# Retention with low-rank expert outputs: one load on another queue, the output weights behind other GpSimd work, and the order of the last unit

## The chip, the cores and the metric

The kernel runs on one core of a Trainium2 chip. Its engines are TensorE (PE in the profile; PEld is its weight loading), VectorE (DVE), ScalarE (ACT), GpSimd (POOL) and SyncE (SP). SP, ScalarE and GpSimd can each issue DMA transfers from their own queue. The metric is the device time of one execution, in microseconds, as the median of several runs; lower is better.

## The reference

There are eight batches (B), eight heads (H), 576 positions (S), head width 64. The first half is attention with a fixed decay instead of a softmax:

```python
scores = scale * np.matmul(q, k.transpose(0, 1, 3, 2))
Dmat = np.where(rel >= 0, gamma[:, None, None] ** rel[None, :, :], 0.0)
ret = scores * Dmat[None, :, :, :]
return np.matmul(ret, v).astype(np.float32)
```

The heads of a position are put side by side into rows x of 512. The second half routes each of the 4608 rows to its two best of eight experts, by `x @ w_gate`, weighs the two by a softmax over their two logits, and adds `weight * (x @ A[e]) @ B[e]` to x. A[e] is 512 x 16 and B[e] is 16 x 512.

## The kernel before

**Tiling.** The sequence is cut into four chunks of 128 positions (NFULL = 4) and one of 64. Since the decay is a power of gamma, the work inside a chunk is a masked product, and what came from earlier chunks is a state P (64 x 64 for each head), which is multiplied by a constant gdec from chunk to chunk. A *unit* is one chunk of two batches with all heads; a *quad* is two units (four batches), and q, k and v of a quad are loaded together by `issue`. There are 18 units, 16 full ones and two of the short chunk. h and n are the last two.

**Stages.** Each unit goes through stages with one-letter names. T transposes q and k on TensorE (result pqT and pkT in PSUM, copied to qT and kT). S multiplies k and q (ps) and applies the mask (rt). Q adds what the state gives, R the product with v (px), and scales it with asc to xT, the attention output, transposed. U forms the new state from scaled k and v (pu, P). Z multiplies xT with AW, which holds the 128 columns of all A[e] and the 8 gate columns (pz), and finds the largest logits on DVE (m, ns). V is a sigmoid on ScalarE (sg). W picks and weighs the two experts (cm, then zc). X transposes zc (pzt, zT). B transposes xT back into the output bank (po). Y adds zT times Bcat, the output weights, to po, copies po to osb and issues the output DMAs.

**What sets the order.** `mm`, `vec` and `act` pass each instruction to `chain` (L73), which writes a fixed program order for PE, DVE and ACT. GpSimd's instructions and the DMAs of SP are not chained: a planner orders them by when they are ready in its own model, with the program's order as priority. PSUM has eight banks, which the kernel hands out itself from a list, oldest first (`bank`, `done`).

**The opening (L227 to L241, L650 to L674).** For the first quad, unit 0's q comes from SP's queue and its k from ScalarE's, one batch each; then v and A (Arow), then unit 1's q, k and v, all from SP (L233). `first_T` transposes unit 0. GpSimd scales k (`scale_k`, L259), builds a selection matrix pick in four dependent steps (`fill_pick`, L622), builds asc[0] and issues two loads: the gate columns of AW[0] (L655) and Bcat (L671). Bcat is converted from fp32 to fp16 by the DMA. ScalarE copies asc[0] into asc[1] with the halves swapped, and expands gdec from its packed form. `place_A` brings A into the layout of AW[0] by matmuls with pick, and GpSimd copies AW[0] into AW[1] with the row halves swapped (L670), once A and the gate columns are both in AW[0]. Stage Z uses AW[0] for its first half and AW[1] for its second. TensorE's order behind `place_A` is: T of unit 1 (q, then k), Z of unit 0, S of unit 1, then U, Q and R of unit 1.

**The end (L764 to L777).** The last two units are short. For n, stage Z is run in two halves, (0,) and (1,), and between them stands Y of h, with its four matmuls, its four copies (two on ScalarE, two on DVE) and its four output DMAs of 128 KB from SP. W of n calls V for a half that has none yet. Y of n, also in halves, issues two of its output DMAs from SP and two from ScalarE.

Of the kernel before, what the change touches and what calls it, by code (L numbers as in the profile page):

```python
# [18 lines left out]
def kernel(  # L19
# [10 lines left out]
    nc = tc.nc  # L30
    B, H, S, Dh = q.shape
# [54 lines left out]
    def act(fn, **kw):  # L86
        chain("act", getattr(nc.scalar, fn)(**kw))  # L87
# [107 lines left out]
    def issue(n):  # L195
        if n >= len(quads):
            return
        c, qd = quads[n]
        first = n == 0
        tl = [  # L200
            iop.tile([128, QUAD, H, Dh], FP32, tag=tag, name=tag, bufs=n)
            for tag, n in (("q32", 2), ("k32", 3), ("v32", 3))
        ]
        if c == NFULL:
            if qd > 0:
                return
            for src, dst in zip((q, k, v), tl):
                for g in range(2):
                    nc.sync.dma_start(
                        out=dst[64 * g : 64 * g + 64].rearrange("p s h d -> p (s h) d"),  # L210
                        in_=src[HALF * g : HALF * g + HALF, :, C * c : C * c + L, :].rearrange(
                            "s h j d -> j (s h) d"
                        ),
                    )
            for u in range(2):
                nat[(c, u, 0)] = [x[:, 2 * u : 2 * u + 2] for x in tl]
            return

        def load(n, lo, hi, eng=nc.sync):
            eng.dma_start(  # L220
                out=tl[n][:, lo:hi].rearrange("p b h d -> p (b h) d"),
                in_=(q, k, v)[n][
                    QUAD * qd + lo : QUAD * qd + hi, :, C * c : C * c + C, :
                ].rearrange("b h j d -> j (b h) d"),
            )

        if first:  # L227
            for b in range(2):
                load(0, b, b + 1)
                load(1, b, b + 1, nc.scalar)  # L230
            load(2, 0, 2)
            load_A()
            for n in range(3):  # L233
                load(n, 2, 4)
        else:
            for n in range(3):
                load(n, 0, 4)
        for sl in range(2):
            nat[(c, qd, sl)] = [x[:, 2 * sl : 2 * sl + 2] for x in tl]
# [7 lines left out]
    def rows(g):  # L247
        return slice(64 * g, 64 * g + 64)
# [4 lines left out]
    def scale_k(t):  # L253

        if not is_full(t):
            return
        kk = nat[units[t]][1]
        for b in range(2):
            gp.tensor_tensor(  # L259
                out=kk[:, b],  # L260
                in0=kk[:, b],
                in1=gv[:, 0].unsqueeze(2).broadcast_to((128, H, Dh)),
                op=ALU.mult,
            )
# [30 lines left out]
    def first_T():  # L295

        s = st.setdefault(0, {})
        for nm in ("qT", "kT"):
            s[nm] = wk.tile([128, 2, HP, C], FP32, tag=nm, name=nm, bufs=4 if nm == "qT" else 2)
        for b in range(2):  # L300
            for n, nm in enumerate(("qT", "kT")):
                src = nat[units[0]][n]
                ps = [bank([128, HP, L], f"p{nm}") for _ in range(2)]
                for hp in range(HP):
                    for g in range(2):
                        mm(
                            ps[g][:, hp, :],
                            lhsT=src[rows(g), b, 2 * hp : 2 * hp + 2, :],
                            rhs=id64[rows(g), :],
                            is_transpose=True,  # L310
                            start=True,
                            stop=True,
                        )
                for g in range(2):
                    o = s[nm][:, b, :, rows(g)]
                    if n == 0:
                        act("copy", out=o, in_=ps[g])
                    else:
                        vec("tensor_copy", out=o, in_=ps[g])
                done(*ps)  # L320
# [146 lines left out]
    def stage_B(t):  # L467

        s = st[t]
        po = [bank([128, 2, HP, Dh], f"po{cc}") for cc in range(2)]  # L470
        for g in range(2):
            for dt in range(HP):
                for cc in range(2):
                    mm(
                        po[cc][:, g, dt, :],
                        lhsT=s["xT"][g][rows(cc), dt, :],
                        rhs=id64[rows(cc), :],
                        is_transpose=True,
                        start=(g == 0 and dt == 0),
                        stop=False,  # L480
                        skip_group_check=True,
                    )
        s["po"] = po
# [136 lines left out]
    def fill_pick(*dts):  # L620
        for dt in dts:
            gp.affine_select(  # L622
                out=pick, in_=pick, compare_op=ALU.not_equal, fill=1.0, base=128 * dt,
                pattern=[[-1, 4], [1, 128]], channel_multiplier=-4,
            )
# [21 lines left out]
    for t in range(NU):  # L647
        if units[t][2] == 0:
            issue(quads.index(units[t][:2]) + 2)
        if t == 0:  # L650
            spin(10)
            first_T()
            scale_k(0)
            fill_pick(3)
            gp.dma_start(  # L655
                out=AW[0][:, :, ER : ER + E], in_=moe_w_gate.rearrange("(t p) e -> p t e", p=128)
            )
            for ho in range(2):
                act("copy", out=asc[1][rows(ho)], in_=asc[0][rows(1 - ho)])
            act(  # L660
                "copy", out=gdec.rearrange("p a b d -> p a (b d)"),
                in_=gde.unsqueeze(2).broadcast_to((128, HP, 2 * Dh)),
            )
            stage_S(0)
            stage_U(0)
            stage_Q(0)
            stage_R(0)
            place_A()
            for ho in range(2):
                gp.tensor_copy(out=AW[1][rows(ho)], in_=AW[0][rows(1 - ho)])  # L670
            gp.dma_start(out=Bcat, in_=moe_B.rearrange("e r d -> (e r) d"))  # L671
            stage_T(1, ("qT",))
            stage_T(1, ("kT",), shared=True)
            scale_k(1)  # L674
            stage_Z(0)
            stage_S(1)
            stage_W(0)
            stage_U(1)
            stage_Q(1)
            stage_R(1)  # L680
            stage_T(2, ("qT",))
            stage_B(0)
            stage_X([0])
            stage_Z(1)
            stage_V(1)
            stage_Y(0, spread=True)
            stage_T(2, ("kT",), shared=True)
            stage_T(3)
            scale_k(2)
            scale_k(3)  # L690
            stage_S(2)
            stage_W(1)
            stage_S(3)
            for u in (2, 3):
                stage_U(u)
                stage_Q(u)
                stage_R(u)
            late_T(4)
            for ho in range(2):
                gp.tensor_tensor(  # L700
                    out=maskh[ho], in0=trih.unsqueeze(1).broadcast_to((128, HP, L)),
                    in1=heads(1, ho, L), op=ALU.mult,
                )
            continue
        if t < 4 or units[t][2] or not is_full(t):
            continue

        before, near = [u for u in (t - 4, t - 3) if u > 0], (t - 2, t - 1)
        here = (t, t + 1)
        for u in here:  # L710
            for b, nm in enumerate(("qT", "kT")):
                stage_S(u, (b,))
                if t > LATE:
                    stage_T(u + 2, (nm,))
            if t > LATE:
                scale_k(u + 2)
        for u in before:
            stage_B(u)
        stage_X(before)
        stage_Z(near[0])  # L720
        stage_V(near[0])
        for u in before:
            stage_Y(u)
        stage_Z(near[1])
        stage_V(near[1])
        if units[t][0] > 0:
            for u in here:
                stage_Q(u)
        for u in near:
            stage_W(u)  # L730
        for u in here:
            stage_U(u)
            if units[t][0] == 0:
                stage_Q(u)
            stage_R(u)
        if t <= LATE:
            late_T(t + 2)
# [28 lines left out]
    stage_X([h])  # L766
    stage_Z(n, (0,))
    stage_V(n, (0,))
    stage_Y(h, spread=True)
    stage_Z(n, (1,))  # L770
    for g in range(2):
        stage_W(n, (g,))
    stage_B(n)
    for g in range(2):
        stage_X([n], (g,))
# [30 lines left out]
```

## Time and profile before

| | |
|---|---|
| median of 8 runs | 185.66 us (184.83 to 187.32) |
| the profiled execution | 187.32 us, span 185.6 us |
| granted TensorE clock, mean over the span | 0.987 |
| busy: PE, PEld, DVE, ACT, POOL | 176.5, 164.9, 115.3, 66.8, 58.2 us |
| DMA | 38.74 MB, mean 209 GB/s |

The span runs from the first to the last instruction; what the execution takes besides (1.7 us here) lies around it. The busy time of an engine counts its instructions, not its waits. In a row of the timeline the columns are start, length, engine, source line, operation, output from inputs, number of instructions; a bracket at its end gives the idle time of the engine before it and what is taken to have ended that. Matmuls, vector and scalar instructions have one line each (L81, L84, L87), since three helpers issue them; they are told apart by their tiles. A row with q behind the engine's name (SPq, ACTq) is the issuing of a DMA from that queue. The rows of DMA issues give the size and the median time from issue to landing.

### The profile page before, as it was taken

To read this page: it belongs to the slowest core of one execution; us is meant where nothing else is said; L and a number is where in the kernel's file an instruction comes from. 1 tells how busy PE (TensorE), PEld (TensorE's weight loads), DVE (VectorE), ACT (ScalarE), POOL (GpSimd) and SP (SyncE) were. 2 spreads that over 40 slices of the span, in tenths; PEclk is the share of its full clock that TensorE was granted. 3 is DMA by queue.
4 is the path that set the end of the run, shared out by engine and by line. 5 is a ranking of instruction groups with operands and counts; after the bars stand their busy time and mean duration, and the time that the engine had idled before them with its cause. 6 is when DMAs were issued, how large, how long until landed. Compare 5 with 4: busy or idle time off the path is not lost. (4 is left out here: it accounts for less than half of the span.)

```text
span 185.6 us, 8103 instructions
## 1 busy us (share of the span) xinstructions
PE 176.5 (95%) x3606; PEld 164.9 (89%) x3606; DVE 115.3 (62%) x294; ACT 66.8 (36%) x179; POOL 58.2 (31%) x69
## 2 busy tenths in 40 slices
PE   7996999999999999999999999999999999999970
PEld 2796998999999999999999999999999999999850
DVE  3784565997578745866267716792578447475660
ACT  3512127024412434097602643075406460132440
POOL 8785106226016600688022710443050004000000
PEclk9998799999999999999999999999999999999998
DMA  6999999997998897899897699999800050033175
GB/s 138 278 255 216 274 271 265 262 309 224 250 280 248 228 295 213 232 350 287 237 316 246 188 296 336 229 215 194 280 4 0 4 222 11 4 112 123 66 247 144
DMA packets 53283, 38.74 MB, mean 209 GB/s; under 512 B 26992, under 2 KB 48640, under 8 KB 53248
## 3 DMA queue, kind: packets, MB, share of 16 engines
q1 hardware_dynamic: 50688, 37.23, 70.7%
q10 hardware_dynamic: 2384, 0.85, 1.9%
q8 instruction: 28, 0.46, 1.0%
q0 software_dynamic: 176, 0.15, 0.5%
q14 instruction: 7, 0.06, 0.1%
HBM read 28.91 MB, written 9.44 MB: 207 GB/s over the span
## 5 line engine op out<-in xcount | busy, mean ns | idle before, releaser
L84 DVE TENSOR_TENSOR rt<-ps,mask 128x512 f32<-128x512 f32 x64 | 40.3, 683 | 9.5 <-PE ps L81 9.2
L259 POOL TENSOR_TENSOR k<-k,pack 128x512 f32<-128x512 f32 x32 | 32.6, 1045 | 27.6 <-PE pkT L81 21.0
L81 PE MATMUL pz<-AW,xT 128*128 128x136 f32 x288 | 38.6, 288 | 0.0
L418 POOL TENSOR_TENSOR P<-pn,gdec 128x512 f32<-128x512 f32 x12 | 15.3, 1279 | 68.7 <-DVE pn L84 64.5
L81 PEld LDWEIGHTS pz<-AW,xT 128*128 128x128 f32 x288 | 35.9, 196 | 0.2
L81 PE MATMUL ps<-qT,kT 64*128 64x128 f32 x512 | 34.2, 280 | 0.1
L81 PEld LDWEIGHTS ps<-qT,kT 64*128 64x128 f32 x512 | 31.0, 189 | 1.3 <-issue 0.9
L81 PE MATMUL px<-rt,v 128*64 128x128 f32 x512 | 30.7, 273 | 0.0
L87 ACT COPY qT<-pqT 128x512 f32<-128x512 f32 (+1 forms) x33 | 16.8, 568 | 31.8 <-PE pqT L81 31.6
L81 PEld LDWEIGHTS px<-rt,v 128*64 128x64 f32 x512 | 27.7, 137 | 0.0
L84 DVE TENSOR_TENSOR xT<-px,asc 128x512 f32<-128x512 f32 x36 | 24.4, 688 | 3.9 <-PE px L81 2.6
L87 ACT COPY kT<-pkT 128x512 f32<-128x512 f32 x29 | 16.0, 600 | 27.5 <-PE pkT L81 18.8
L84 DVE COPY lg<-pz 128x16 f32<-128x16 f32 x17 | 2.9, 173 | 34.3 <-PE pz L81 34.3
L81 PE MATMUL pu<-v,k 128*64 128x64 f32 x512 | 18.1, 224 | 0.0
L87 ACT COPY osb<-po 128x256 f32<-128x256 f32 x60 | 17.5, 386 | 1.4 <-PE po L81 0.8
L87 ACT ACTIVATE sg<-lg,ns 128x8 f32<-128x8 f32 x34 | 8.4, 293 | 26.4 <-DVE ns L84 26.1
L81 PEld LDWEIGHTS pu<-v,k 128*64 128x64 f32 x512 | 16.6, 138 | 1.4 <-issue 1.0
L81 PE MATMUL pkT<-id,k 64*128 64x64 f32 x288 | 12.9, 227 | 1.8 <-DVE qT L84 1.4
L81 PE MATMUL px<-qT,P 64*64 64x128 f32 (+1 forms) x512 | 14.1, 259 | 0.0
L81 PEld LDWEIGHTS pkT<-id,k 64*128 64x128 f32 x288 | 11.4, 141 | 2.9 <-DVE qT L84 1.5
L84 DVE TENSOR_TENSOR pn<-pu,P 128x512 f32<-128x512 f32 x12 | 8.3, 692 | 8.3 <-PE pu L81 8.3
L81 PEld LDWEIGHTS px<-qT,P 64*64 64x64 f32 x512 | 12.5, 133 | 0.9
(54 smaller groups left out, 150.5 us busy)
## 6 DMA issues: line engine op xcount, KB each, us to landing
out_dram<-osb SPq DMA_DIRECT2D x32, 256.0 KB, 3.8
v<-in_v_dram SPq DMA_DIRECT2D x4, 512.0 KB, 7.7
q<-in_q_dram SPq DMA_DIRECT2D x3, 512.0 KB, 5.8
k<-in_k_dram SPq DMA_DIRECT2D x3, 512.0 KB, 7.9
out_dram<-osb SPq DMA_DIRECT2D x6, 128.0 KB, 2.3
q<-in_q_dram SPq DMA_DIRECT2D x2, 256.0 KB, 4.2
k<-in_k_dram ACTq DMA_DIRECT2D x2, 256.0 KB, 4.8
Arow<-in_moe_A_dram SPq DMA_DIRECT2D x1, 256.0 KB, 6.5
```

What stands on the lines that cost most here:

```text
L81: chain("pe", nc.tensor.matmul(*args, **kw))
L84: chain("dve", getattr(nc.vector, fn)(**kw))
L87: chain("act", getattr(nc.scalar, fn)(**kw))
L259: gp.tensor_tensor(out=kk[:, b], in0=kk[:, b], in1=gv[:, 0].unsqueeze(2).broadcast_to((128, H, Dh)), op=ALU.mult,)
L418: nc.gpsimd.tensor_tensor(out=Pt, in0=pn, in1=gdec, op=ALU.mult)
```

## The change

Three things are changed.

1. Unit 1's k is loaded from ScalarE's queue, chained behind ScalarE's copies of `first_T`, instead of from SP between q and v. The expansion of gdec goes from ScalarE to GpSimd, in the program ahead of the last step of pick.
2. The two AW[1] copies and the load of Bcat are chained on GpSimd in this order.
3. In the last unit, the second half of Z and its V come directly behind the first; W of both halves follows, and Y of h comes behind these, ahead of B of n.

```diff
         def load(n, lo, hi, eng=nc.sync):
-            eng.dma_start(
+            return eng.dma_start(
...
             load(2, 0, 2)
             load_A()
-            for n in range(3):
-                load(n, 2, 4)
+            load(0, 2, 4)
+            load(2, 2, 4)
+            nat["k of unit 1"] = lambda: chain("act", load(1, 2, 4, nc.scalar))
...
             spin(10)
             first_T()
+            nat["k of unit 1"]()
             scale_k(0)
+            gp.tensor_copy(
+                out=gdec.rearrange("p a b d -> p a (b d)"),
+                in_=gde.unsqueeze(2).broadcast_to((128, HP, 2 * Dh)),
+            )
             fill_pick(3)
...
                 act("copy", out=asc[1][rows(ho)], in_=asc[0][rows(1 - ho)])
-            act(
-                "copy", out=gdec.rearrange("p a b d -> p a (b d)"),
-                in_=gde.unsqueeze(2).broadcast_to((128, HP, 2 * Dh)),
-            )
...
             for ho in range(2):
-                gp.tensor_copy(out=AW[1][rows(ho)], in_=AW[0][rows(1 - ho)])
-            gp.dma_start(out=Bcat, in_=moe_B.rearrange("e r d -> (e r) d"))
+                chain("pool", gp.tensor_copy(out=AW[1][rows(ho)], in_=AW[0][rows(1 - ho)]))
+            chain("pool", gp.dma_start(out=Bcat, in_=moe_B.rearrange("e r d -> (e r) d")))
...
     stage_Z(n, (0,))
     stage_V(n, (0,))
-    stage_Y(h, spread=True)
     stage_Z(n, (1,))
+    stage_V(n, (1,))
     for g in range(2):
         stage_W(n, (g,))
+    stage_Y(h, spread=True)
     stage_B(n)
```

## The prediction

> **What bounds the kernel now.** I read the engine totals first, then the opening by order of time, the granted clock by window, the transfers' landing times, and the tail by order of time. The totals:
>
> ```profile
> PE 176.5 (95%) x3606; PEld 164.9 (89%) x3606; DVE 115.3 (62%) x294; ACT 66.8 (36%) x179; POOL 58.2 (31%) x69
> PEclk9998799999999999999999999999999999999998
> ```
>
> TensorE is busy for 176.5 of 185.6 us, and the list of its waits leaves little to win outside both ends: between 15.84 and 178.9 us its only idle entry is one of 0.28. The clock row dips once, in the fourth and fifth slices (13.9 to 23.2 us). So a change pays by what it does to the first 21 us, or after 177 us. The opening:
>
> ```profile
> 7.84 2.01 SPq L220 DMA_DIRECT2D k<-in_k_dram  x1
> ...
> 9.47 0.64 POOL L622 TENSOR_SCALAR_AFFINE_SELECT pick<-pick 128x512 f32<-128x512 f32 x1
> ...
> 10.06 0.94 POOL L655 DMA_DIRECT2D AW<-in_moe_w_gate_dram  x1
> ...
> 11.01 0.65 POOL L622 TENSOR_SCALAR_AFFINE_SELECT pick<-pick 128x512 f32<-128x512 f32 x1
> 11.59 0.57 POOL L671 DMA_DIRECT2D Bcat<-in_moe_B_dram  x1
> ...
> 13.69 0.71 PE L81 MATMUL pqT<-id,q 64*128 64x64 f32 x16
> ...
> 15.84 0.71 PE L81 MATMUL pkT<-id,k 64*128 64x64 f32 x16 [1.44 <-DVE qT L84]
> 16.03 1.31 POOL L670 COPY AW<-AW 64x544 f32<-64x544 f32 x2 [2.65 <-DMA AW<-in_moe_w_gate_dram]
> ...
> 16.48 3.17 PEld L81 LDWEIGHTS pz<-AW,xT 128*128 128x128 f32 x16
> ```
>
> TensorE stands still from 14.40 to 15.84 before unit 1's k transposes. The row names DVE's qT copies, but by the code's bank list pkT takes the two banks that unit 0's px gave back at 13.40 us (end of the xT copies). What lands then is k itself:
>
> ```profile
> k<-in_k_dram SPq DMA_DIRECT2D x1, 512.0 KB, 7.9
> ```
>
> Issued at 7.84, landed at 7.84 + 7.9 = 15.74. Its q lands at 6.94 + 4.9 = 11.84. After the gap the clock falls:
>
> ```profile
> 16.50:17.00 0.50, 0.50 (x6) 0.50 (x5) 0.41 (x1) 0.44 (x1) 0.46 (x2) 1.00 1.04 156
> ...
> 18.00:18.50 0.50, 0.50 (x4) 0.50 (x4) 0.00 (x0) 0.00 (x0) 0.50 (x2) 0.50 1.06 352
> ```
>
> (Window and its length; us of PE, PEld, DVE, ACT, POOL; clock; DMA share; GB/s.) It is 0.50 from about 17.0 to 20.4. Unit 0's sixteen pz matmuls take 3.49 us there and 2.07 at full clock for unit 1: 1.42 lost, some 1.5 with the first ps.
>
> **Start, k on ScalarE's queue.** The issue comes behind the qT copies, which end at 7.75: not earlier than the 7.84 of before. What changes is the ring. The nearest row is unit 0's second k, also from ScalarE's queue beside a backlog on SP: issued 1.85, landed after 5.4. That gives 13.2 for k. The Trainium skill speaks against this edit ("DMA: Bandwidth & Descriptors", Issuing engines are not separate DMA queues): all queues share the same DMA engines and interleave. The DMA share is 1.0 to 1.3 here, so the trace agrees that k's bytes come out of q's share: q, 2.0 us of transfer behind k at worst, lands at up to 13.9 instead of 11.84, against a first use at 13.69. By the row both transposes are done at 13.9 + 2 x 0.71 = 15.3, often a little sooner; if the rule meant no gain at all, k would land at 15.7 as before. The sum below hardly depends on which, because of the next edit. ScalarE pays an issue of 0.9 (the same size on SP) to 2.0 us; the asc copies (1.25) end by 11.1 against a use near 12.6. If that cover failed, unit 0's second xT would be late. SP issues v about 2 us sooner, behind the same bytes: nothing.
>
> **Start, gdec on GpSimd.** ScalarE loses 0.62; it was idle until 13.77, so nothing is gained. GpSimd's copy takes about 0.63 (64x544 took 0.636). Its place matters. GpSimd has no written order, and its rows show what the planner does: pick steps, which depend on each other, alternate with something ready (asc, k, k, then the gate weights' load between the last two picks). gdec, always ready and in front of that load in the program, takes that slot; then the last pick is ready and also in front. So I expect pick 9.47, gdec 10.1, pick 10.7, gate load at 10.06 + 0.63 + 0.64 = 11.3. gdec is there for unit 0's P at 11.26, with 0.5 to spare. The load:
>
> ```profile
> AW<-in_moe_w_gate_dram POOLq DMA_DIRECT2D x1, 16.0 KB, 5.8
> ```
>
> It lands at 11.3 + 5.8 = 17.1. All of pz(0) waits for it, and its second half for the two AW copies behind it (1.31), at 18.5. Before, it landed at 15.86 and had 0.6 us of cover under the k transposes; that cover is gone. So the wait for k turns into a wait for the gate weights, from 15.3 to 17.2, and pz starts 0.7 later than 16.48. The bounds: if the planner puts the load where it was, pz can start at 16.0 (0.5 gained); with one more ring to share, 6.5 instead of 5.8 makes it 1.4 lost. I take 0.7.
>
> **The clock.** The Trainium skill ("TensorE: Matmul & The Clock Gate", Part 1) wants an idle window of about 3.4 us for the drop, so by it neither 1.44 nor 2 us of standing would cost anything, and the new start would run at full clock: 1.5 less, partly eaten by the AW copies (first half 17.2 to 18.2, second 18.5 to 19.6). The row has the drop after 1.44 us; with the transposes on both sides it is 13.69 to 16.48, 2.8 us without an ordinary matmul (2.2 us of bare transposes at 40.03 cost no clock). After the change the stretch is 13.7 to 17.2, 3.5 us, so I keep the drop. Then pz takes 3.5 again, ending at 20.7 against 19.97, and the AW copies hide under its slow first half. Start: +0.7.
>
> **Bcat later.** It frees 128 KB of transfers before 18 us and asks for them later. Issued behind the AW copies at 18.5, it lands at 19.1 + 6.3 = 25.4; first use was 28.14. It holds GpSimd for 0.57, so unit 1's k scaling ends at 18.5 + 0.57 + 2.04 = 21.1, needed by pu at 22.14 + 0.7. Zero; if both covers failed, under 1 us.
>
> **Tail.** Before:
>
> ```profile
> 177.35 0.76 DVE L84 COPY osb<-po 128x256 f32<-128x256 f32 x2
> 177.37 0.27 ACT L87 ACTIVATE sg<-pz,ns 128x8 f32<-128x8 f32 x1 [0.81 <-PE po L81]
> 177.54 0.64 ACT L87 COPY osb<-po 128x256 f32<-128x256 f32 x2
> 177.93 4.21 SPq L606 DMA_DIRECT2D out_dram<-osb  x6
> ...
> 178.28 0.17 DVE L84 MAX8 m<-pz 128x8 f32<-128x8 f32 x1 [0.17 <-PE pz L81]
> ...
> 179.30 0.29 DVE L84 TENSOR_TENSOR zc<-pz,cm 128x128 f16<-128x128 f32 x1
> ...
> 181.67 0.50 ACTq L606 DMA_DIRECT2D out_dram<-osb  x1
> ```
>
> Four po matmuls (0.44 of PE) leave the front of the last pz, which then ends at 177.80, not 178.24. DVE, in its written order: m at 177.83, ns, two pairs of cm and zc at 0.25 a step: last zc ends at 179.1, not 179.59. The compute chain gains some 0.3 us behind ScalarE's two copies. But Y(h) carries four output DMAs, and they move with it: DVE's two osb copies now stand behind zc, and the first ends at 179.5, not 177.77. SP issued its six at 177.93, 178.53, 179.27, 179.86, 180.66 and 181.67: about 0.63 apart when nothing holds it. From 179.55 the sixth starts at 179.55 + 5 x 0.63 = 182.7 and lands 2.5 later (its landing before), 185.2. The last landing before is ScalarE's, 181.67 + 2.8 = 184.47. So +0.7. Below: if SP issues at its fastest row (0.35, the pair at 176.31) the end is the compute chain, -0.3. Above: these eight transfers of 128 KB ran at some 210 GB/s; all queued from 179.55, 5 us of transfer after 1.1 of start-up ends near 185.7, +1.2. I take +0.7, the row of the same transfers.
>
> **Sum.** The profiled execution took 187.32 (span 185.6, 1.7 around it): 187.32 + 0.7 + 0.7 = 188.7. It lies 1.66 above the median of 185.66, and the eight runs reach from 184.83 to 187.32. My reading is that the clock loss of 1.5 is not in every run of before; with the longer gap it will be in most runs of after. So I take off 1.0, not 1.66: **187.7 us**.
>
> **Rivals and chances.** One run to the next a kernel like this moves by about 1%, and less than that can't be told from no change.
> - Forecast, 0.58: 187.7, own range 186.6 to 189.0.
> - The gate load keeps its place, 0.25. For: gdec might fill GpSimd's idle 5.5 to 6.9. Against: the planner took k there. pz starts 0.5 sooner, the clock loss comes half the time (-0.7), tail +0.7: 186.8 on the profile's scale, 185.6 on the median's with 1.2 off.
> - k does what is meant and nothing follows, 0.09, the faster side. The one mechanism is unbroken TensorE work from q's transposes into pz: 1.44 + 1.5 gone, and the tail's 0.3: 187.32 - 3.2 = 184.1, which has no clock loss left to take off. It decides from a gate landing at 15.1 or sooner; no row shows one under 5.8 us.
> - Two windows of lost clock and SP at the upper bound, 0.08: 187.7 + 1.5 = 189.2.
> - The change does not bring k sooner: possible by the skill's rule, same time as the forecast.
>
> Slower than 187.52 are about two thirds of the forecast and the fourth case, 0.48; faster than 183.8 half of the third at best, 0.05. The range leaves out a tenth on each side: 184.8 to 189.2.
>
> **What would show it.** Right: the gate load issued after gdec and the last pick, near 11.3; an idle entry of TensorE at pz(0), 1.5 to 2.2 us, with DMA AW named; clock 0.50 behind it; SP's first output of Y(h) near 179.5 plus the shift of the start, and SP's last landing as the end. Wrong: a gate load before 10.5, a full clock through 21 us, or SP's last issue within 0.3 of ScalarE's.

## The result

The changed kernel takes 186.73 us (median of 11 runs, 185.89 to 190.93); the kernel before, run beside it and with the earlier runs 32 times in all, 184.89 us (183.92 to 187.32). The ratio is 1.0097, with a 95% interval of 1.0064 to 1.0130: slower by 1%, some 1.8 us. The profiled execution of the changed kernel took 186.92 us with a span of 185.2. That its span is 0.4 shorter than the 185.6 of before says little: the profiled execution of before was, at 187.32, the slowest of its 32 runs. It had the clock loss behind the opening, and this one has not. So the two traces are compared stretch by stretch here.

The totals and the clock row of the changed kernel's page:

```profile
PE 175.0 (94%) x3606; PEld 163.1 (88%) x3606; DVE 115.8 (63%) x294; ACT 66.2 (36%) x178; POOL 58.8 (32%) x70
...
PEclk9999999999999999999999999999999999999995
```

The same matmuls; TensorE's busy time is 1.5 less, since the clock stayed up behind the opening (unit 0's pz and unit 1's ps are busy for 2.35 and 2.06 us here, 3.49 and 2.31 before). The opening by order of time:

```profile
7.00 0.37 ACTq L220 DMA_DIRECT2D k<-in_k_dram  x1
...
9.39 0.64 POOL L623 TENSOR_SCALAR_AFFINE_SELECT pick<-pick 128x512 f32<-128x512 f32 x1
...
9.97 0.61 POOL L656 COPY gdec<-pack 128x512 f32<-128x512 f32 x1
10.53 0.64 POOL L623 TENSOR_SCALAR_AFFINE_SELECT pick<-pick 128x512 f32<-128x512 f32 x1
...
11.11 0.94 POOL L661 DMA_DIRECT2D AW<-in_moe_w_gate_dram  x1
...
14.43 0.67 PE L81 MATMUL pkT<-id,k 64*128 64x64 f32 x16
...
16.56 1.16 PE L81 MATMUL pz<-AW,xT 128*128 128x136 f32 x8 [1.46 <-DMA AW<-in_moe_w_gate_dram]
...
17.83 0.59 POOL L673 DMA_DIRECT2D Bcat<-in_moe_B_dram  x1
17.94 0.99 PEld L81 LDWEIGHTS pz<-AW,xT 128*128 128x128 f32 x8 [0.41 <-POOL AW L672]
...
19.06 2.06 PE L81 MATMUL ps<-qT,kT 64*128 64x128 f32 x32
```

The wait before the k transposes is gone: k was there, 5.3 us after its issue at 7.00, and pkT follows pqT at 14.43. In its place stands a wait of 1.46 before pz(0), for the gate columns. GpSimd does gdec and the last pick step ahead of their load, which is issued at 11.11 instead of 10.06. pz(0) starts at 16.56; before, it was 16.48. The second half of pz waits once more, for the copies into AW[1]: from the first pz to unit 1's ps it is 2.50 us (16.56 to 19.06), against 2.05 (16.34 to 18.39) in the run with Bcat alone below, which has neither this wait nor the clock loss.

The tail by order of time:

```profile
174.29 2.07 PE L81 MATMUL pz<-AW,xT 128*128 128x136 f32 x16
...
177.43 0.29 DVE L84 TENSOR_TENSOR zc<-pz,cm 128x128 f16<-128x128 f32 x1
...
177.90 1.09 DVE L84 COPY osb<-po 128x256 f32<-128x256 f32 x3 [0.17 <-issue]
...
178.38 3.79 SPq L607 DMA_DIRECT2D out_dram<-osb  x6
...
179.12 1.36 ACTq L607 DMA_DIRECT2D out_dram<-osb  x2
179.34 0.42 DVE L84 COPY osb<-po 128x256 f32<-128x256 f32 x1 [0.36 <-PE po L81]
```

And of before, the two rows that the comparison needs besides those shown ahead:

```profile
175.73 1.15 PE L81 MATMUL pz<-AW,xT 128*128 128x136 f32 x8
...
181.27 0.37 ACT L87 COPY osb<-po 128x256 f32<-128x256 f32 x1 [0.79 <-PE po L81]
```

Both halves of n's Z are now one row of sixteen. Counted from the first pz of n, the last osb copy ends after 5.47 us (179.76 - 174.29), where it was 5.91 (181.64 - 175.73): the computing is 0.44 faster. But the first output of h is issued 4.09 after that point (178.38) instead of 2.20 (177.93), and the span ends after 10.91 us instead of 9.87: the tail is 1.04 longer.

### The profile page after: what moved, and what is told of

It reads as the page before. It is cut to its first block, busy times and chain, and to the rows that moved or that the text cites. A ratio compares the mean times of both kernels' runs of the same rounds, so it can differ in the third digit from the quotient of the medians.

```text
span 185.2 us, 8103 instructions
## 1 busy us (share of the span) xinstructions
PE 175.0 (94%) x3606; PEld 163.1 (88%) x3606; DVE 115.8 (63%) x294; ACT 66.2 (36%) x178; POOL 58.8 (32%) x70
## 5 line engine op out<-in xcount | busy, mean ns | idle before, releaser
L81 PE MATMUL pz<-AW,xT 128*128 128x136 f32 x288 | 37.3, 282 | 1.7 <-DMA AW<-in_moe_w_gate_dram 1.5
L81 PEld LDWEIGHTS pz<-AW,xT 128*128 128x128 f32 x288 | 34.7, 190 | 2.1 <-ACT kT L87 1.6
L81 PEld LDWEIGHTS pkT<-id,k 64*128 64x128 f32 x288 | 11.3, 141 | 1.7 <-DMA k<-in_k_dram 0.7
```

The lines of the kernel that those rows point to most:

```text
L81: chain("pe", nc.tensor.matmul(*args, **kw))
```

## The experiments

"Before" in the ratios is the kernel before, run on the same chip beside each. Ratios with their intervals are compared, not medians, since the chips differ by some tenths of a microsecond.

**The tail alone.** The kernel before with

```diff
-    stage_Y(h, spread=True)
     stage_Z(n, (1,))
+    stage_V(n, (1,))
     for g in range(2):
         stage_W(n, (g,))
+    stage_Y(h, spread=True)
```

> The kernel before with the change's tail alone (opening as before). Theory of the output queue: the four output DMAs of Y(h) start some 1.7 us later against the start of the last Z, SP issues six at 0.6 to 0.65 us apart, and the last landing moves out by about 1.1 us although the last osb copy is some 0.4 us sooner: 1.1 us over the kernel before. Rival, that the whole loss sits in the opening: 0.3 to 0.4 us under the kernel before, with the last landing from ScalarE's queue.

Measured: 1.0053 (1.0015 to 1.0090), 1.0 us. In its trace the span ends 10.92 us after the first pz of n, as in the change. So the tail carries about half of the loss.

**The opening alone.** The change with the tail of before:

> The change with the tail of before put back (opening as changed). Theory of the gate weights: TensorE has no wait before unit 1's k transposes any more but one of about 1.5 us before pz(0), named after the load of AW; against the kernel before 0.4 to 0.8 us slower, 1.1 us faster than the change. Rival, that k on ScalarE's queue brings its gain and the tail alone costs: 1 us or more faster than before.

Measured: 1.0039 (1.0011 to 1.0068), 0.7 us. Together the two halves give 0.92%, the change 0.97%. The wait for the gate columns was there, but only 0.30 in this trace, not 1.5: the load was issued at 10.96 and landed after 4.5 us. The landing differs from execution to execution (below).

**Is it who issues the outputs?** The change with two of h's four outputs issued by GpSimd instead of SP:

```diff
-                q_ = nc.scalar if last and x == 1 else nc.sync
+                q_ = (nc.scalar if last else gp if t == NU - 2 else nc.sync) if x == 1 else nc.sync
```

> The change with h's two output DMAs of the second batch issued by GpSimd instead of SP, so that SP issues four at the end and not six. Theory of the output queue: SP's last issue starts near 180 us of a span like the change's and not 181.6, the end follows the last osb copy, and 1.0 to 1.4 us come back. Rival, that the transfers and not the issues are the limit (about 1 MB at some 210 GB/s from the first start): within 0.4 us of the change.

Measured: 1.0117 (1.0060 to 1.0175, from six runs), no faster than the change. The tail by order of time, then by windows (window and its length; us of PE, PEld, DVE, ACT, POOL; clock; DMA share; GB/s):

```profile
180.01 3.20 SPq L607 DMA_DIRECT2D out_dram<-osb  x4
...
180.54 1.12 POOL L607 DMA_DIRECT2D out_dram<-osb  x2 [22.19 <-ACT osb L87]
...
180.75 1.37 ACTq L607 DMA_DIRECT2D out_dram<-osb  x2
```

```profile
183.00:184.00 1.00, 0.00 (x0) 0.00 (x0) 0.00 (x0) 0.00 (x0) 0.00 (x0) 1.00 1.03 283
184.00:185.00 1.00, 0.00 (x0) 0.00 (x0) 0.00 (x0) 0.00 (x0) 0.00 (x0) 0.63 0.99 357
```

SP had four issues and not six, the last of them 6.03 us after the first pz of n (175.92) instead of 7.31, and the span still ended 10.78 us after it, 0.13 less than the change. From 183 to 185 us nothing computes and the DMA share is 1.0; the last landing comes 3.55 us after SP's last issue. So in this run the transfers hold the end.

That doesn't clear SP's issues in the change itself. There the last landing comes 2.52 us after SP's last issue, at 181.60, and the first of h's outputs took 2.32 us from issue to landing: the last transfer hardly queued. And the run brings a load of its own. Of 181 to 186 us its queues took (packets, MB, share of the 16 engines):

```profile
q0 software_dynamic: 96, 0.26, 24.7%
q10 hardware_dynamic: 160, 0.26, 14.9%
```

GpSimd's two transfers (q0) kept the engines busy longer than ScalarE's two of the same size (q10), by an estimated 0.5 us of all sixteen (9.8% of 5 us). By this reading the two limits, SP's issues and the transfers, lie close together: with one eased, the other holds the end.

**Is it the bytes?** The change without two of h's four outputs:

```diff
-            for x in range(2):
+            for x in range(1 if t == NU - 2 else 2):
                 n0 = S * (HALF * g + 2 * qd + x) + C * c
```

> The change, leaving out h's output of its second batch (two of its four DMAs of 128 KB), so that SP issues four and 256 KB less are written at the end. Theory, that the transfers queued at the end are the limit and not who issues them: 0.7 to 1.2 us faster than the change, that is within 0.4 us of its opening's cost over the kernel before. Rival, that the end hangs on a fixed time behind the last osb copy: less than 0.3 us faster than the change.

Measured: 1.0037 (1.0011 to 1.0062), 0.6 points under the change, 1.1 us. That is the cost of the opening alone. Its trace, with a quarter of the last megabyte gone, ends 10.12 us after the first pz of n: 0.79 of the tail's 1.04 are back. The last osb copy ends 5.46 us after that point, as in the change (5.47), so its place decides nothing: the outputs of h that start late hold the end. The run takes away two of SP's issues along with their bytes (SP's last issue comes 6.02 us after the first pz of n), so which of the two counts in the change stays open.

**The gate columns first.** The change's opening, the tail of before, and the load of the gate columns ahead of pick:

```diff
+    gp.dma_start(
+        out=AW[0][:, :, ER : ER + E], in_=moe_w_gate.rearrange("(t p) e -> p t e", p=128)
+    )
     gp.memset(pick, 0.0)
     fill_pick(0, 1)
...
             fill_pick(3)
-            gp.dma_start(
-                out=AW[0][:, :, ER : ER + E], in_=moe_w_gate.rearrange("(t p) e -> p t e", p=128)
-            )
```

> The change's opening with the load of the gate columns issued by GpSimd before it sets pick to zero (near 2.7 us), and the tail of before. Theory of the gate weights: they are there long before unit 1's transposes end, pz(0) starts at 15.2 to 15.5 us with no wait over 0.3 us, AW[1] is copied by about 16.2; 1.0 to 1.4 us faster than the kernel before. Rival, that pz(0) is held by something else as well (the A part of AW, k itself): a wait of over 1 us stays before pz(0) and the time is that of the opening as changed.

Measured: 0.9971 (0.9942 to 1.0000), 0.5 us faster than before. In its opening the load is issued at 2.74 and TensorE goes through:

```profile
2.74 0.94 POOL L628 DMA_DIRECT2D AW<-in_moe_w_gate_dram  x1
...
14.47 0.67 PE L81 MATMUL pkT<-id,k 64*128 64x64 f32 x16
...
14.91 1.31 POOL L672 COPY AW<-AW 64x544 f32<-64x544 f32 x2 [2.88 <-issue]
...
15.07 1.19 PE L81 MATMUL pz<-AW,xT 128*128 128x136 f32 x8
```

pz(0) starts at 15.07, 1.4 us sooner than before, as the theory has it. The time has less than half of that.

**gdec back on ScalarE.** The change's opening with gdec on ScalarE, as before, and the tail of before:

```diff
-            gp.tensor_copy(
+            act(
-                out=gdec.rearrange("p a b d -> p a (b d)"),
+                "copy", out=gdec.rearrange("p a b d -> p a (b d)"),
```

> The opening as changed but gdec expanded on ScalarE again, and the tail of before: k on ScalarE's queue and Bcat late, with the gate columns' load back between GpSimd's third and last pick step, near 10.1 us. Theory, that gdec's place on GpSimd delays that load: it lands about 1 us sooner than in the opening as changed (11.0 to 11.1 issue there), pz(0) starts 0.5 to 1.0 sooner, and the time is within 0.4 us of the kernel before, on the faster side. Rival, that the third queue beside it makes the load slow: issue near 10.1, but landing no sooner than 15.9, and 0.4 to 0.8 us slower than before, as with the whole opening.

Measured: 0.9999 (0.9965 to 1.0033). The load is issued at 9.40, pz(0) starts at 15.16 after a wait of 0.23. The cost of the opening goes away with gdec, though the interval overlaps that of the opening alone, and no gain appears. In this trace the list of TensorE's waits between 22 and 176 us has

```profile
PE pkT L81 <- DMA k<-in_k_dram: 1.7, 1, 1.7
```

a wait for a later quad's k (at 81.97), where the trace of before has none.

**gdec alone.** The kernel before with only gdec moved to GpSimd, as in the change:

> The kernel before with gdec expanded on GpSimd ahead of the last pick step, and nothing else. Theory of the gate weights' issue: issued near 11.2 us, landing about 16.5 to 17, just behind the k transposes (16.5): pz(0) waits 0 to 0.6, the second half of pz for the AW[1] copies a little: 0.2 to 0.7 us slower than before. Rival, that this load's place doesn't matter: no wait before pz(0), no difference.

Measured: 1.0048 (1.0011 to 1.0086), 0.9 us. The size is right, but this execution's trace doesn't show the reason: the load was issued at 10.63, landed after 4.2 us, ahead of pz(0) at 15.15, and TensorE lost its time at 38.73 (1.28, k of a later quad) and in two short stops. That the later load is the cause rests on two other pairs: gdec back on ScalarE takes the opening's cost away, and gdec on GpSimd costs nothing once the load is ahead of it (0.9971 against 0.9974 in the last run of this section).

The traces don't size this cost. In the four with the changed opening unit 1's ps starts at 17.47 (half of h's outputs), 18.14 (the opening alone), 19.06 (the change) and 20.82 us (two queues); in three with k and the gate columns as before at 18.39 (Bcat alone), 18.55 (the tail alone) and 19.90 (before). Two of the four are ahead of all three. So the runs show which edit costs the 0.7 us; that the wait for the gate columns is how it costs them is argued.

**Filling the stall.** The kernel before with three matmuls of 512 columns on the idle tile between unit 1's q and k transposes:

```diff
-            stage_T(1, ("kT",), shared=True)
+            stage_T(1, ("kT",), shared=True, fill=3)
```

> The kernel before with three 512-wide matmuls of the idle tile (some 0.43 us each) into the bank of unit 1's k transposes, between q's and k's transposes, where TensorE stood 1.1 to 1.4 us. Theory, that the clock falls in some executions because of that stretch without ordinary matmuls: the stall is filled, no execution loses clock before 21 us, the median is 0.3 to 0.8 us under the kernel before. Rival, that the clock loss has another cause (or plays no part in the median): the median as before or up to 0.3 slower.

Measured: 1.0033 (1.0007 to 1.0059). TensorE is busy without a break from 12 to 24 us and the clock stays at 1.00 in its trace, but the median is higher, not lower. The filler has a cost of its own: k landed at 15.79 in this trace, and its transposes start at 16.10, behind the filler. So a small gain from the clock can't be ruled out, but none shows. This trace, the slowest of the kernel's 22 runs, also has waits for later k's (1.66 at 40.4 and 0.56 at 84.4).

**Bcat alone.** The kernel before with the AW[1] copies and Bcat's load chained on GpSimd:

> The kernel before with the load of Bcat chained behind the AW[1] copies, and nothing else. My working: no cost and no gain, within 0.3 us of the kernel before; Bcat lands near 24 us, ahead of its use near 27. Rival, that its 128 KB in front of unit 1's k matter: k lands about 0.5 us sooner, the wait before the k transposes shrinks by that, 0.3 to 0.6 us faster.

Measured: 1.0010 (0.9978 to 1.0042), nothing. k landed 8.0 us after its issue at 7.57, as before.

**The gate columns first, k from SP.** The kernel before with the load ahead of pick:

> The kernel before with the gate columns' load issued by GpSimd ahead of pick's memset; k stays on SP's queue. Theory of two waits in series: k still holds the k transposes to near 15.8, pz(0) follows at once as before, no difference (within 0.3 us). Rival, that the gate columns alone were the limit: 0.5 us or more faster.

Measured: 1.0028 (0.9999 to 1.0056), not faster. In this execution k was early (the transposes start at 14.83 without a wait; it landed 6.8 us after its issue; with gdec alone it was 6.7, in the other four traces with k on SP 7.2 to 8.0), so the trace doesn't show k as the holder; the runs show that the gate columns alone bring nothing.

**Two edits only.** The kernel before with k on ScalarE's queue and the gate columns first; gdec, Bcat and tail as before:

> The kernel before with two edits only: unit 1's k on ScalarE's queue and the gate columns' load ahead of pick's memset; gdec on ScalarE, Bcat and the tail as before. Theory of two waits in series: with both taken away pz(0) starts at 15.0 to 15.5 without a wait, and the time is 0.4 to 1.2 us under the kernel before, though later loads may take part of it back as waits for k in the middle of the span. Rival, that the late Bcat was needed for it: not faster than before.

Measured: 0.9974 (0.9948 to 0.9999). pz(0) at 15.11 without a wait, no wait of TensorE between 22 and 176 us in the trace, span 182.8. With the run of the gate columns first, the gain of 0.3% over the kernel before stands twice. Each time the interval only just ends at 1.

## Why the prediction was right, and where it was not

- **k lands sooner on the other queue.** Right: 12.3 us (7.00 + 5.3) against a forecast of 13.2 and 15.74 before; q moved to 13.5 (6.80 + 6.7), forecast at most 13.9; in the run with two queues it came at 14.2, and its transposes waited 0.62 us for it. The issue came at 7.00, not behind the qT copies at 7.75: it was recorded ahead of the last copy, which starts at 7.22, and took 0.37 instead of 0.9 to 2.0.
- **gdec takes the slot of the gate columns' load.** Right: gdec at 9.97, pick at 10.53, load at 11.11, forecast 10.1, 10.7, 11.3.
- **The wait for k becomes one for the gate columns.** Right in kind, with DMA AW named and 1.46 us. pz(0) started 0.1 later than before, not 0.7, because the load was issued 0.2 sooner than forecast and landed after 5.3 and not 5.8 us. The forecast took one landing time from one trace; in the four traces with this opening it is 4.2 to 5.9 us. Over many runs the opening costs 0.7 us (0.39%), the forecast's +0.7. That agreement is partly luck: the forecast had the clock loss on both sides, with the AW[1] copies hidden under it, and the traces don't show a steady 0.7.
- **The clock.** Wrong, and it was a term of the sum: the full clock through 21 us, named as a sign of being wrong, is in the trace. The step said that the loss "will be in most runs of after" and so took off only 1.0 of the 1.66 us between profile and median. Of the four traces with the changed opening one has the loss, the run with two queues, where the stretch between ordinary matmuls was 3.5 us as forecast; in the other three it was 1.2, 1.5 and 2.7 (13.87 to 16.56 in the change), since the gate columns landed sooner. Of the three with the opening as before, one has it, before itself, with 2.8; the run with Bcat alone has 2.86 (13.48 to 16.34) and no loss. So the length alone doesn't decide it between 2.7 and 2.9; what does is open. The rule of an idle window of about 3.4 us in the Trainium skill ("TensorE: Matmul & The Clock Gate", Part 1) is no worse a guide here than the one row that the forecast set against it, though it doesn't explain the loss of before. Taking off the full 1.66 would have given 187.1.
- **Bcat.** Right: zero. It landed at 24.0 (17.83 + 6.2), used at 27.19.
- **The tail.** Right in sign, mis-sized: +1.04 for +0.7. SP's six issues took place nearly as worked out (178.38 to 181.60, forecast 178.1 to 181.3 once the start's shift of -1.44 is put in), and the last landed 2.5 us later, as worked out. The 0.3 that is missing is the later first issue and steps of 0.64 for 0.63. What the working had as its upper bound, all eight transfers queued behind a late start, lies close behind: taking two issues from SP gained only 0.13.
- **The sum.** For start and tail 1.4 us was forecast, and 1.8 measured. Against the median the forecast was +2.0 (187.7 less 185.66), of which 0.66 stood for a clock loss in more runs. That share didn't come, and the tail cost 0.3 more, so the nearness of 2.0 to 1.8 is partly luck. The forecast of 187.7 lies 1.0 above the measured 186.73, by the clock's share and by a median of before that was 185.66 in eight runs and 184.89 in 32.

## What to carry to other kernels

When a load that is waited for is brought forward, look up the next one that the same instruction or its follower needs: here k and the gate columns landed within about a microsecond of each other (15.7 and 15.9 before), and either alone brought nothing. A small copy moved to an idle engine is not free if a DMA is issued behind it on that engine's queue: here it cost 0.4 to 0.5%. At the end of a kernel, output that is ready early should be issued early, even if that costs the compute chain some tenths: here the chain was 0.44 faster and the end 1.04 later.

## What the runs showed of the hardware

- **The 16 KB load of the gate columns lands anywhere from 4.2 to 6.1 us after its issue** in the traces here, beside loads that keep the DMA share at 1.0 or above. A start fixed by such a landing moves by over a microsecond between executions, and one profile can't size it.
- **Small outputs issued one by one from SP ran at half the rate.** At the end of the changed kernel, and in before under its outputs of 256 KB (columns as above):

```profile
180.00:180.50 0.50, 0.00 (x0) 0.00 (x0) 0.00 (x0) 0.00 (x0) 0.00 (x0) 1.00 0.85 201
...
181.50:182.00 0.50, 0.00 (x0) 0.00 (x0) 0.00 (x0) 0.00 (x0) 0.00 (x0) 0.50 1.01 369
```

```profile
177.50:178.00 0.50, 0.50 (x7) 0.50 (x5) 0.50 (x2) 0.50 (x3) 0.00 (x0) 1.00 1.03 393
```

  While SP's outputs of 128 KB (64 partitions) follow each other alone the engines are 85% busy for 201 GB/s; from 181.5 to 183.5 us, with ScalarE's two beside them for half of it, the mean is 321. SP issued one every 0.64 us, an issue taking 0.54 to 0.59, which allows an estimated 204 GB/s from its queue alone; before's last four issues of 256 KB (128 partitions) took 0.33 to 0.49. The half rate is not a matter of 64 partitions as such: in before, from 182.50 to 182.75 us, ScalarE's outputs of 64 partitions had 97% of the engines' time almost alone, at 377 GB/s.
- **The middle of the span differs more than both ends.** From unit 1's ps to the first pz of n the thirteen traces take 155.1 to 158.5 us (the change 155.2, before 155.8), though no edit is to an instruction there. Three of them have a wait of 1.3 to 1.7 us for a later quad's k, at 38.73, 40.4 and 81.97. A sooner opening moves TensorE towards such waits, so part of its gain can go there; that the missing half of the 1.4 us went there is argued, not shown, since the two faster kernels' traces have no such wait.
